# Extra drains on GpSimd, another block order at the end, a smaller first load, and two reorderings in the last turns of a gated scan with a routed expert layer

## The chip, the cores and the metric

One core of a Trainium2 chip runs the whole program. The metric is the device time of one execution in microseconds, and the median of three runs of the kernel before is 382.46 us (382.41 to 382.51). The engines are named as in the profile: PE is TensorE's matmuls, PEld its weight loads, DVE is VectorE, ACT is ScalarE, POOL is GpSimd, SP is SyncE. A q behind a name (POOLq) marks what the engine's sequencer does by itself: waits, branches, drains.

## The reference

A recurrent state with a forget gate for each row, and then a layer of eight experts of which each token uses one.

```python
# q, k, v, f_logit: (4, 8, 768, 48)
f = sigmoid(f_logit)
for t in range(768):
    state = f[:, :, t, :, None] * state + einsum('bhd,bhe->bhde', k[:, :, t], v[:, :, t])
    y[:, :, t] = einsum('bhd,bhde->bhe', q[:, :, t], state)
x = y.transpose(0, 2, 1, 3).reshape(3072, 384)

logits = x @ w_gate                      # 8 experts
e_idx = argmax(logits)
gate_w = softmax(logits)[e_idx]
eom = sigmoid(x @ w_output_gate)
for e in range(8):
    h = maximum(x[e_idx == e] @ w1[e], 0)     # 384 -> 1024
    out[e_idx == e] = gate_w * eom[:, e] * (h @ w2[e])
```

## The kernel before, in words

**The scan.** Four batches of 768 tokens are cut into chunks of 128: 24 turns, one for each chunk, all eight heads together. `prep(t)` makes what turn `t` needs: the sigmoid of the forget gates (`f` and `s`, on ACT), the running product `p` of the gates and its inverse `i` (`scan_p` and `scan_i`, on DVE), and the products `k * i` and `q * p` (`mul_k` and `mul_q`; from turn 3 on both on GpSimd). In turn `t` the function `attention` multiplies k and q of the chunk (`qk`, PE), masks the square (`mask`: one half by DVE, the other by an ACT copy and a GpSimd select), transposes k (`kn_tr`), forms the output of chunk `t - 1` from the state and the masked square (`out_y`), adds the chunk to the state (`state` on PE, `state_upd` on DVE), and transposes the output of chunk `t - 2` into token order together with its gate logits (`x_tr`, PE; `evac_x`, ACT). `evac_y` copies an output from PSUM.

**Loads.** `load(b, cuts)` issues the loads of one batch on SyncE's queue: a cut ("fqk", 0, 2) stands for the gates, q and k of chunks 0 and 1. In the first two batches a load of two chunks has 512 KB, in pieces of 1 KB (256 tokens of 4 bytes). The transfers move in the order in which they are issued.

**Routing.** `route` finds the expert of each token of a group (eight groups, `RG`), by DVE operations that are handed out a few at a time. `slots` counts on PE and DVE where each token goes; `run_pq` runs it. `scatter(n)` then sends up to n chunks of 128 tokens to their places in `xs_dram`, by one indirect DMA each, issued by GpSimd. From turn 20 on (`T_END`) up to four chunks are sent in a turn. Once 16 chunks are sent (`T_TOP`), `tokens_in(0, 0, 2)` loads the first 256 tokens of the largest expert (`first_x`, SyncE); this load waits until those 16 scatters have landed. `x_early` transposes them on PE and splits them into two parts.

**The last turn** (`t == last`) has an order of its own: after `out_y(22)` and `state(22)` it runs the pending slots, sends two chunks, then copies `y` of turn 22, updates the state, does `x_early`, and forms `out_y(23)`, for half of the heads at a time.

**The experts.** `Experts.run` takes the experts in order of size, the largest first. Weights are loaded by SyncE when a buffer is free and split into a high and a low part; each product is three matmuls (`mm1` from 384 to 1024, `mm2` back). For experts 0 to 5 the output of expert s is transposed, scaled by ACT and scattered to `out` during expert s + 1 (`put`, four blocks). Experts 6 and 7 use `mm2_rows`: three blocks of up to 128 tokens, of which each is scaled (half by ACT, then half by DVE, since the second reads the same PSUM bank) and scattered at once. So 30 output blocks are scattered. Every scatter is an indirect DMA of GpSimd and waits for the landing of the one before, since both write to `out`. The scaled blocks have three buffers.

**The end.** `check` counts whether the fast method was valid, into the register `bad`. `tc.If(bad > 0)` would run `general_path`, a slow method for all tokens; with these inputs it is skipped. Behind it comes the closing code (recorded on line 1130): every engine drains, SyncE waits for the outstanding DMAs one by one, and GpSimd releases a barrier of all engines.

**What sets the order.** Each engine runs its instructions in the order in which the program writes them (`chain` ties the order of DVE, ACT, GpSimd and PE); SyncE's queue is in the order of its calls.

Of the kernel before, what the change touches and what calls it, by code (L numbers as in the profile page):

```python
# [13 lines left out]
AF = mybir.ActivationFunctionType  # L14
ALU = mybir.AluOpType
# [112 lines left out]
def attention(ctx, tc, nc, k, kpool, rt, q01, k01, f01, q23, k23, f23, v, wg, xs_dram, r, ex):  # L128
# [40 lines left out]
    def load(b, cuts):  # L169
        i = b % 2  # L170
        if b not in v_t:
            v_t[b] = vp.tile([128, NCH, H * 64], F32, name="v_t")
        src = {"f": (f_t[i], f01, f23), "k": (k_t[i], k01, k23), "q": (q_t[i], q01, q23)}
        for what, c0, c1 in cuts:
            sl = slice(c0 * C, c1 * C)
            for w in what:
                if w == "v":
                    nc.sync.dma_start(out=v_t[b][:, c0:c1, :], in_=v[b, sl].rearrange("(c p) h e -> p c (h e)", p=C))
                    continue
                t, first, rest = src[w]  # L180
                if b < 2:
                    nc.sync.dma_start(out=t[:, :, sl], in_=first[b, :, :, sl].rearrange("g p s -> p g s"))
                else:
                    for par in range(2):
                        nc.sync.dma_start(out=t[64 * par:64 * par + D, :, sl],
                                          in_=rest[b - 2, par::2, :, sl].rearrange("h d s -> d h s"))
# [171 lines left out]
    def run_pq(n=None):  # L358
        n = len(pq) if n is None else n
        todo, pq[:] = pq[:n], pq[n:]  # L360
        for f in todo:
            f()
# [58 lines left out]
    order = [(b, c) for b in range(B) for c in range(NCH)]  # L421
    last = len(order) - 1
    pre_of = [prep(t) for t in range(len(order))]
    load(0, [("fqk", 0, 2), ("f", 2, 4), ("v", 0, 2), ("qk", 2, 4)])
    nc.sync.dma_start(out=turn[:, 0::2, 2 * D:XW], in_=wg[:, 0::2, 0:2 * E])
    for i in range(2):
        nc.sync.dma_start(out=turn[64 * i:64 * i + 64, 1::2, 2 * D:XW],
                          in_=wg[64 - 64 * i:128 - 64 * i, 1::2, 0:2 * E])
    load(0, [("v", 2, 4), ("fkqv", 4, 6)])
    load(1, [("fkqv", 0, 2), ("fkqv", 2, 4), ("fkqv", 4, 6)])  # L430
    for e in range(E):
        ex.clear(e)
# [29 lines left out]
    for t in range(last + 1):  # L462
        ready = len(pq)
        more = 1 if t < T_END else 0

        fill(more)
        if hot(t - 2):
            evac_y(t - 2, (1,))
        if t not in (0, 2):
            pre(t + 2, "f")  # L470
        if hot(t - 2):
            evac_y(t - 2, (0,))
            state_upd(t - 2)
        if t == 2:
            pre(4, "f")
        pre(t + 1, "mul_k")
        if t + 1 == last:
            done_sb.close()
            ex.open_early()
        fill(more)  # L480
        if t > 1:
            pre(t + 2, "scan_p")
        qk(t)
        mask(t, 1)
        mask(t, 0)
        if t == 0:
            pre(2, "s", "f")
        pre(t + 2, "scan_p", "scan_i")
        if t == 0:
            pre(2, "mul_k")  # L490
        fill(more)
        kn_tr(t)
        if t == 0:
            warm_up(nc, k, one, 4)
        if hot(t - 2):
            x_tr(t - 2)
        evac_kn(t)
        pre(t + 2, "mul_q", "ends")
        if hot(t - 2):
            evac_x(t - 2)  # L500
        if t == last:
            ex.split(1, 0, 1, nc.gpsimd)
        fill(more)
        if T_END <= t < last:
            fill(8)
        pre(t + 3, "s")
        if t == last:
            done_ps.close()
            ex.open_early_psum()
        if hot(t - 1):  # L510
            out_y(t - 1)
        if hot(t - 1):
            state(t - 1)
        run_pq(ready)
        if t == last:
            scatter(2)

            evac_y(t - 1)
            state_upd(t - 1)
            ex.x_early()  # L520
            for heads in ((0, 1, 4, 5), (2, 3, 6, 7)):
                out_y(t, heads)
            ex.split(1, 0, 2, nc.gpsimd)
        if t >= T_SCAT:
            scatter(1 if t < T_END else 2)

        b, c = divmod(t - 3, NCH)
        if t >= 3 and b + 2 < B and c in (0, 2, 4):
            load(b + 2, [("fkq", c, c + 2)])
            if c == 4:  # L530
                load(b + 2, [("v", i, i + 2) for i in range(0, NCH, 2)])
        fill(2 if more else 10)
        fill(2 * more)
        if t - 2 in ends:
            route(*ends[t - 2])
        if t >= T_END:
            scatter(2)
            if len(ex.apart) == T_TOP:
                ex.tokens_in(0, 0, EARLY // TS)
                ex.load_rest(0)  # L540
        if t + 1 == last:
            drain()
            assert ex.xg
            ex.split(1, 0, 0, nc.gpsimd)
# [32 lines left out]
class Experts:  # L577
# [208 lines left out]
    def mm2_rows(self, s, step):  # L786

        k, nc = self.k, self.nc
        for j, n in self.rows(s):
            ps = self.psy.tile([128, 512], F32, name=f"y_ps{j}")  # L790
            i = 0
            for f in range(KF):
                wh, wl = self.whl[2, s, f // 2]
                hh, hl = (t[:, j * TS:j * TS + n] for t in self.hs[s, f][0])
                for a, b in ((hh, wh), (hl, wh), (hh, wl)):
                    nc.tensor.matmul(ps[0:n, 0:DM], a, b[:, f % 2, :], start=(i == 0), stop=(i == 3 * KF - 1))  # L796
                    i += 1
                step(j * KF + f)
            t = self.yp.tile([TS, DM], F32, name="o", bufs=3)
            half = DM // 2  # L800
            nc.scalar.activation(out=t[0:n, 0:half], in_=ps[0:n, 0:half], func=AF.Copy,
                                 scale=k.gain[0:n, j, s:s + 1])
            nc.vector.tensor_scalar(out=t[0:n, half:DM], in0=ps[0:n, half:DM], scalar1=k.gain[0:n, j, s:s + 1],
                                    scalar2=None, op0=ALU.mult)
            self.scatter(s, j, n, t)

    def y_out(self, s):
# [56 lines left out]
    def run(self):  # L864
        step = self.step
        step(len(self.todo))
        self.load_rest(1)
        for f in range(AHEAD):
            if f == AHEAD - 2:
                self.x_late()  # L870
            self.mm2(0, f)
        for s in range(E):
            if s > 0 and s + 1 < E:
                self.load(s + 1, self.k.number[0:1, s + 1:s + 2])
            back = self.rows(s - 1) if s > 0 and len(self.rows(s - 1)) > KC else []
            if s == 0:
                later = self.meta.pop()
                self.gains()
                self.meta = [later]
            for f in range(KF):  # L880
                self.mm1(s, f)
                if s == 0:
                    self.gain(2)
                    if f in (3, 5):
                        self.split(1, 1, f // 2 - 1)
                if f % 2 == 0 and (2, s, f // 2) in self.wr:
                    self.split(2, s, f // 2, self.nc.gpsimd if s == 0 else None)
                if 1 <= f <= len(back):
                    self.put(s - 1, *back[f - 1])
            front = [lambda i=i: self.split(1, s + 1, i) for i in range(KF // 2)  # L890
                     if (1, s + 1, i) in self.wr]
            for c in range(KC):
                front.insert(2 * c + 2 if s > 0 else 2 * c + 1, lambda c=c: self.x_in(s + 1, c))
            if s + 1 == E:
                front = []
            self.gain(len(self.gq))
            self.gains()
            if len(self.rows(s)) <= KC:
                self.mm2_rows(s, lambda i: self.gain(1) if i % 3 != 1 else front.pop(0)() if front else None)
                self.gain(len(self.gq))  # L900
                continue
            for f in range(KF):
                for part in range(len(self.hs[s, f])):
                    if not (s == 0 and part == 0 and f < AHEAD):
                        self.mm2(s, f, part)
                if front:
                    front.pop(0)()
                self.gain(2)
                if s == 1:
                    step(1)  # L910
            self.gain(len(self.gq))
            self.y_out(s)
            if s == 0:
                self.todo += check(self.nc, self.k, self.r, self.kp, self.pso)
# [151 lines left out]
def tile_kernel(ctx: ExitStack, tc: tile.TileContext, q01, k01, f01, q23, k23, f23, v, vT, wg, wgn, w1, w2, out):  # L1066
# [20 lines left out]
    def part(first, rest):  # L1087
        return lambda b, h: first[b, h // 2, 64 * (h % 2):64 * (h % 2) + D, :] if b < 2 else rest[b - 2, h]

    with tc.If(bad > 0):  # L1090
        general_path(tc, nc, part(q01, q23), part(k01, k23), part(f01, f23), vT, wgn, w1, w2, y_dram, out)


# [40 lines left out]
```

## Time and profile before

| | us |
|---|---|
| median of the runs | 382.46 |
| the profiled execution's own time | 382.55 |
| its span, first to last instruction | 380.8 |
| PE busy | 361.7 (95%) |
| DVE busy | 234.8 (62%) |
| ACT busy | 196.8 (52%) |
| POOL busy | 146.7 (39%) |

The profile is of one execution. Busy is the time in which an engine worked, waits and branches left out. The chain of waits goes back from the last instruction, at each step to what released it; its shares say where the span was decided. A row of a timeline gives the start and the duration in us, the engine, the line, the operation, the tiles (output <- inputs) and, in brackets, how long the engine was idle before and what ended that.

### The profile page before, as it was taken

Reading aid. Unit: us, or ns where it says so; the run is one execution under the profiler, and the core shown is the slowest. Engines: PE = TensorE matmul, PEld = TensorE weight load, DVE = VectorE, ACT = ScalarE, POOL = GpSimd, SP = SyncE. Lnnn points to the kernel's source line nnn. Section 1 sums busy time; section 2 is a strip of 40 time slices with the busy share of each in tenths; the row PEclk is TensorE's granted clock in tenths of the full one; section 3 lists DMA queues with packets and bytes.
Section 4 is the critical chain, followed back from the end, with each engine's and each line's share of the span. In section 5 each row is a group of like instructions: output and inputs, shape, how many; then the busy total and the mean of one; then the engine's idle time right before and its main releaser. Section 6 shows DMA issues by size and latency. Waiting matters only on the chain.

```text
span 380.8 us, 8463 instructions
## 1 busy us (share of the span) xinstructions
PE 361.7 (95%) x3199; PEld 334.2 (88%) x3199; DVE 234.8 (62%) x488; ACT 196.8 (52%) x468; POOL 146.7 (39%) x176
## 2 busy tenths in 40 slices
PE   7899999999998999999999999999999999999990
PEld 2688988898986999899989999999999999999980
DVE  6988989898974655645535545644653654665410
ACT  3576866866756434446336435625634644744310
POOL 6686698999988630002102201301210211231021
PEclk9999999999999999999999999999999999999996
DMA  8999999999178149545453543545444454420010
GB/s 253 348 359 359 312 252 267 299 269 284 47 244 265 54 148 335 177 133 167 134 170 124 175 126 126 167 127 185 133 162 135 159 166 128 160 66 35 2 43 21
DMA packets 51843, 67.75 MB, mean 178 GB/s; under 512 B 3906, under 2 KB 46421, under 8 KB 51792
## 3 DMA queue, kind: packets, MB, share of 16 engines
q1 hardware_dynamic: 48480, 57.46, 50.6%
q0 software_dynamic: 3312, 9.65, 7.0%
q8 instruction: 27, 0.44, 0.5%
q14 instruction: 24, 0.20, 0.2%
HBM read 54.16 MB, written 13.39 MB: 177 GB/s over the span
## 4 chain that ended last, share of the span: by engine, by line
PE 78%; DVE 9%; ACT 3%; issue 3%; DMA 3%; POOL 2%; POOLq 0%; DVEq 0%; ACTq 0%
PE h_ps L760 28%; PE y_ps L782 22%; PE x_ps L322 5%; PE y_ps L796 4%; PE a_ps L245 3%; PE x_ps L710 3%; PE two_ps L309 2%; DVE p L209 2%; DVE i L216 2%; PE o_ps L817 2%; PE two_ps L305 2%; PE one_ps L309 2%; PE kn_ps L262 2%; PE one_ps L278 2%; DMA out<-o,dst 2%
## 5 line engine op out<-in xcount | busy, mean ns | idle before, releaser
L825 POOL DMA_INDIRECT out<-o,dst x30 | 31.7, 1058 | 187.8 <-ACT o L820 118.6
L765 DVE SCALAR_TENSOR_TENSOR hl<-h_ps,hh 128x256 fp32r<-128x256 f32 (+6 forms) x72 | 39.3, 547 | 51.2 <-ACT hh L764 50.8
L760 PE MATMUL h_ps<-xh,w1h 128*128 128x400 f32 (+6 forms) x192 | 67.4, 351 | 0.3 <-DVE hl L765 0.3
L760 PE MATMUL h_ps<-xh,w1l 128*128 128x400 f32 (+6 forms) x192 | 65.0, 338 | 0.0
L760 PE MATMUL h_ps<-xl,w1h 128*128 128x400 f32 (+6 forms) x192 | 65.0, 338 | 0.0
L764 ACT ACTIVATE hh<-h_ps 128x256 fp32r<-128x256 f32 (+6 forms) x72 | 34.8, 484 | 50.1 <-PE h_ps L760 48.5
L782 PE MATMUL y_ps<-hh,w2h 128*128 128x256 f32 (+4 forms) x168 | 57.7, 343 | 0.0
L782 PE MATMUL y_ps<-hl,w2h 128*128 128x256 f32 (+4 forms) x168 | 55.7, 331 | 0.0
L782 PE MATMUL y_ps<-hh,w2l 128*128 128x256 f32 (+4 forms) x168 | 55.6, 331 | 0.0
L717 DVE TENSOR_TENSOR xl<-x_ps,xh 128x400 fp32r<-128x400 f32 (+6 forms) x23 | 13.1, 569 | 41.8 <-ACT xh L716 38.4
L760 PEld LDWEIGHTS h_ps<-xh,w1h 128*128 128x128 f32 x192 | 36.1, 188 | 1.2 <-DVE hl L765 0.6
L716 ACT CAST xh<-x_ps 128x400 fp32r<-128x400 f32 (+6 forms) x23 | 11.3, 490 | 48.9 <-PE x_ps L710 42.3
L760 PEld LDWEIGHTS h_ps<-xl,w1h 128*128 128x128 f32 x192 | 36.1, 188 | 0.4
L760 PEld LDWEIGHTS h_ps<-xh,w1l 128*128 128x128 f32 x192 | 36.0, 188 | 0.5
L636 DVE TENSOR_TENSOR w2l<-w2r,w2h 128x768 fp32r<-128x768 f32 x31 | 30.7, 989 | 4.2 <-ACT w2h L635 1.3
L223 POOL TENSOR_TENSOR q_t<-q_t,p 128x512 f32<-128x512 f32 x24 | 30.6, 1276 | 6.1 <-DVE p L209 5.9
L245 PE MATMUL a_ps<-q_t,k_t 64*128 64x128 f32 x384 | 28.4, 285 | 4.5 <-DVE k_t L220 2.7
L782 PEld LDWEIGHTS y_ps<-hh,w2h 128*128 128x128 f32 x168 | 31.6, 188 | 1.1
L782 PEld LDWEIGHTS y_ps<-hl,w2h 128*128 128x128 f32 x168 | 31.6, 188 | 0.5
L782 PEld LDWEIGHTS y_ps<-hh,w2l 128*128 128x128 f32 x168 | 31.7, 189 | 0.4
L209 DVE TENSOR_TENSOR_SCAN p<-f_ps,start_p 128x511 f32<-128x511 f32 x22 | 28.0, 1274 | 4.0 <-ACT start_p L197 2.4
L245 PEld LDWEIGHTS a_ps<-q_t,k_t 64*128 64x128 f32 x384 | 23.7, 187 | 7.1 <-POOL q_t L223 2.0
(176 smaller groups left out, 773.4 us busy)
## 6 DMA issues: line engine op xcount, KB each, us to landing
w1r<-in_w SPq DMA_DIRECT2D x32, 384.0 KB, 3.7
w2r<-in_w SPq DMA_DIRECT2D x32, 384.0 KB, 3.2
v_t<-in_v SPq DMA_DIRECT2D x12, 512.0 KB, 8.6
xg<-xs_dram SPq DMA_DIRECT2D x5, 802.0 KB, 5.0
xs_dram<-empty SPq DMA_DIRECT2D x8, 401.0 KB, 10.9
f_t<-in_f SPq DMA_DIRECT2D x6, 512.0 KB
q_t<-in_q SPq DMA_DIRECT2D x6, 512.0 KB, 9.4
k_t<-in_k SPq DMA_DIRECT2D x6, 512.0 KB, 8.6
```

The costliest lines, as they stand in the source:

```text
L209: nc.vector.tensor_tensor_scan(out=flat(d["p"])[:, 1:n], data0=flat(d["f"])[:, 0:n - 1], data1=sp[:, 1:n], initial=sp[:, 0:1], op0=ALU.mul ...
L223: nc.gpsimd.tensor_tensor(out=q_t[i][:, :, sl], in0=q_t[i][:, :, sl], in1=d["p"], op=ALU.mult)
L245: nc.tensor.matmul(aps[t][par][:, g, :], k_t[b % 2][r, g, sl], q_t[b % 2][r, g, sl], start=(g == 0), stop=(g == NP - 1))
L309: nc.tensor.matmul(yps[t][g % 2][r0:r0 + 64, g // 2, :], v_t[b][:, c, 64 * h:64 * h + 64], at[t][:, h % 2, g, :], start=(c == 0 and h < 4) ...
L322: nc.tensor.matmul(xps[t][:, g, :], xt[t][:, g, :], turn[:, g, :], start=(g == 0), stop=(g == NP - 1))
L636: (eng or self.nc.vector).tensor_tensor(out=flat(lo), in0=flat(t), in1=flat(hi.bitcast(F32)), op=ALU.subtract)
L760: nc.tensor.matmul(ps[:, 0:n], a[:, c, cs], b, start=(i == 0), stop=(i == 3 * KC - 1))
L764: nc.scalar.activation(out=hi, in_=ps[:, 0:n], func=AF.Relu)
L765: nc.vector.scalar_tensor_tensor(out=lo, in0=ps[:, 0:n], scalar=0.0, in1=hi.bitcast(F32), op0=ALU.max, op1=ALU.subtract)
L782: self.nc.tensor.matmul(self.ys[d][:, c0:c0 + n], a[:, f % 2, ds], b, start=(f == 0 and i == 0 and part == 0), stop=(f == KF - 1 and i == ...
L796: nc.tensor.matmul(ps[0:n, 0:DM], a, b[:, f % 2, :], start=(i == 0), stop=(i == 3 * KF - 1))
L825: self.nc.gpsimd.indirect_dma_start(out=self.out, out_offset=bass.IndirectOffsetOnAxis(ap=self.k.dst[0:n, j, s:s + 1], axis=0), in_=t[0:n] ...
```

## The change

Six edits. The first load takes chunk 0 alone, then chunks 1 and 2, then 3 and 4, and chunk 5 with the second part. In the last turn the copy of `y(22)` and the state update come ahead of the pending slots and the two scatters. In turns 20 and 21 `mul_k` of turn t + 2 is done ahead of that turn's scatters (it was done at the start of the turn after). `mm2_rows` scales a block with one ACT instruction over all 384 columns. From expert 2 on, GpSimd gets a drain at the start of each expert (six drains). And the conditional block at the end is laid out so that the arm that skips `general_path` comes next in the program.

```diff
@@ -421,12 +421,12 @@
     order = [(b, c) for b in range(B) for c in range(NCH)]
     last = len(order) - 1
     pre_of = [prep(t) for t in range(len(order))]
-    load(0, [("fqk", 0, 2), ("f", 2, 4), ("v", 0, 2), ("qk", 2, 4)])
+    load(0, [("fqk", 0, 1), ("fqk", 1, 3), ("v", 0, 2), ("fqk", 3, 5)])
     nc.sync.dma_start(out=turn[:, 0::2, 2 * D:XW], in_=wg[:, 0::2, 0:2 * E])
     for i in range(2):
         nc.sync.dma_start(out=turn[64 * i:64 * i + 64, 1::2, 2 * D:XW],
                           in_=wg[64 - 64 * i:128 - 64 * i, 1::2, 0:2 * E])
-    load(0, [("v", 2, 4), ("fkqv", 4, 6)])
+    load(0, [("v", 2, 4), ("fkq", 5, 6), ("v", 4, 6)])
     load(1, [("fkqv", 0, 2), ("fkqv", 2, 4), ("fkqv", 4, 6)])
     for e in range(E):
         ex.clear(e)
@@ -511,16 +511,20 @@
             out_y(t - 1)
         if hot(t - 1):
             state(t - 1)
-        run_pq(ready)
-        if t == last:
-            scatter(2)
+        if t < last:
+            run_pq(ready)
+        else:
 
             evac_y(t - 1)
             state_upd(t - 1)
+            run_pq(ready)
+            scatter(2)
             ex.x_early()
             for heads in ((0, 1, 4, 5), (2, 3, 6, 7)):
                 out_y(t, heads)
             ex.split(1, 0, 2, nc.gpsimd)
+        if T_END <= t:
+            pre(t + 2, "mul_k")
         if t >= T_SCAT:
             scatter(1 if t < T_END else 2)
 
@@ -797,11 +801,7 @@
                     i += 1
                 step(j * KF + f)
             t = self.yp.tile([TS, DM], F32, name="o", bufs=3)
-            half = DM // 2
-            nc.scalar.activation(out=t[0:n, 0:half], in_=ps[0:n, 0:half], func=AF.Copy,
-                                 scale=k.gain[0:n, j, s:s + 1])
-            nc.vector.tensor_scalar(out=t[0:n, half:DM], in0=ps[0:n, half:DM], scalar1=k.gain[0:n, j, s:s + 1],
-                                    scalar2=None, op0=ALU.mult)
+            nc.scalar.activation(out=t[0:n], in_=ps[0:n, 0:DM], func=AF.Copy, scale=k.gain[0:n, j, s:s + 1])
             self.scatter(s, j, n, t)
 
     def y_out(self, s):
@@ -872,6 +872,8 @@
         for s in range(E):
             if s > 0 and s + 1 < E:
                 self.load(s + 1, self.k.number[0:1, s + 1:s + 2])
+            if s > 1:
+                self.nc.gpsimd.drain()
             back = self.rows(s - 1) if s > 0 and len(self.rows(s - 1)) > KC else []
             if s == 0:
                 later = self.meta.pop()
@@ -1087,7 +1089,7 @@
     def part(first, rest):
         return lambda b, h: first[b, h // 2, 64 * (h % 2):64 * (h % 2) + D, :] if b < 2 else rest[b - 2, h]
 
-    with tc.If(bad > 0):
+    with tc.If(bad > 0, preferred_fallthrough_block=False):
         general_path(tc, nc, part(q01, q23), part(k01, k23), part(f01, f23), vT, wgn, w1, w2, y_dram, out)
```

## Rows read from the trace of the kernel before

**Rows 1.** The page, part 4: shares of the chain of waits by engine.

```profile
PE 78%; DVE 9%; ACT 3%; issue 3%; DMA 3%; POOL 2%; POOLq 0%; DVEq 0%; ACTq 0%
```

**Rows 2.** Timelines of ACT, DVE and POOL, 369 to 381 us.

```profile
370.53 0.42 ACT L801 ACTIVATE o<-y_ps,gain 120x192 f32<-120x192 f32 x1 [3.73 <-PE y_ps L796]
...
370.99 0.42 DVE L803 TENSOR_SCALAR o<-y_ps,gain 120x192 f32<-120x192 f32 x1 [3.73 <-ACT o L801]
...
372.21 1.03 POOL L825 DMA_INDIRECT out<-o,dst  x1 [3.70 <-DVE o L803]
```

**Rows 3.** Instructions on the tile o, 372 to 381 us: issue to landing.

```profile
DMA to landing us min/median/max: 3.0/3.0/3.0
```

**Rows 4.** Line 1130: op xcount, ns min/median/max, first and last start.

```profile
L1130 POOLq DRAIN  x3: 40/107/4492, 375.5 to 380.6; - x3
...
L1130 SPq DRAIN  x3: 7/7/12, 375.9 to 380.3; - x3
...
L1130 DVEq DRAIN  x2: 10/72/135, 377.3 to 380.3; - x2
```

**Rows 5.** The same view of line 1125, the program's start.

```profile
L1125 POOLq DRAIN  x1: 176/176/176, 0.4 to 0.4; - x1
```

**Rows 6.** Timeline of POOL, 318 to 323 us.

```profile
322.72 1.09 POOL L825 DMA_INDIRECT out<-o,dst  x1 [15.77 <-ACT o L820]
```

**Rows 7.** The view of line 1090, the branch at the end.

```profile
L1090 PEldq COMPARE_BRANCH  x1: 3722/3722/3722, 367.8 to 367.8; - x1
...
L1090 POOLq COMPARE_BRANCH  x1: 53/53/53, 372.5 to 372.5; - x1
...
L1090 POOLq EVENT_SEMAPHORE  x1: 17/17/17, 375.4 to 375.4; - x1
```

**Rows 8.** Chain of waits, 361 to 381 us: start, us, what.

```profile
363.80 2.58 DMA out<-o,dst
...
367.53 3.83 DMA out<-o,dst
```

**Rows 9.** DMA queues, 367.6 to 371.4 us: packets, MB, share.

```profile
q8 instruction: 1, 0.02, 2.1%
```

**Rows 10.** Instructions on the tile o, whole span: ns min/median/max.

```profile
L820 ACT ACTIVATE o<-o_ps,gain x24: 569/578/588, 169.3 to 327.9; 128x384 f32<-128x384 f32 x19, 16x384 f32<-16x384 f32 x2, 64x384 f32<-64x384 f32 x1, 48x384 f32<-48x384 f32 x1
```

**Rows 11.** Chain of waits, 0 to 6 us.

```profile
0.80 4.21 DMA f_t<-in_f
...
5.86 1.29 DVE p L209
```

**Rows 12.** Busy time by stretch; the last number is GB/s.

```profile
5.00:7.50 2.50, 2.50 (x13) 1.15 (x12) 1.57 (x3) 1.93 (x7) 1.19 (x16) 1.00 1.09 354
...
9.00:10.00 1.00, 0.56 (x10) 0.59 (x11) 1.00 (x2) 0.00 (x0) 0.00 (x0) 1.00 1.04 377
```

**Rows 13.** Timelines of DVE and ACT in the first turns.

```profile
9.26 1.27 DVE L209 TENSOR_TENSOR_SCAN p<-two_ps,start_p 128x511 f32<-128x511 f32 x1
...
14.41 0.20 ACT L197 ACTIVATE start_p<-f_t 128x4 f32<-128x4 f32 x1
```

**Rows 14.** Waits, 109 to 116 us: total, times, longest.

```profile
PE a_ps L245 <- POOL k_t L220: 1.5, 2, 0.8
```

**Rows 15.** Timelines of POOL, SP and PE in the last turns.

```profile
107.28 0.98 POOL L339 DMA_INDIRECT xs_dram<-xn,slot  x1 [0.30 <-issue]
...
113.85 1.29 POOL L220 TENSOR_TENSOR k_t<-k_t,i 128x512 f32<-128x512 f32 x1
...
114.40 0.37 SPq L657 DMA_DIRECT2D first_x<-xs_dram  x1
...
119.85 0.63 PE L710 MATMUL x_ps<-ident,first_x 128*128 128x128 f32 x4
...
121.19 0.65 PE L305 MATMUL f_ps<-q_t,state 64*64 64x128 f32 x8 [0.49 <-DVE state L293]
```

**Rows 16.** Instructions on the tile first_x, 114 to 118 us: issue to landing.

```profile
DMA to landing us min/median/max: 5.1/5.1/5.1
```

## The prediction

> **What bounds the kernel now.** I read the chain of waits first, then the sequencers' instructions at the end, then the first 15 us and the last turns of the scan. The chain is TensorE for 78% of the span [rows 1]: from the third turn of the scan to the end of the last expert nothing but a shorter wait of PE can pay. That leaves three places where PE does not set the time: the head (the first forget gates are waited for), the last four turns (PE waits for GpSimd's `k` product), and the tail after PE's last matmul, 370.5 to 380.8 us. The change touches all three.
>
> The tail is the largest. The last ACT and DVE scaling end at 371.4, the last scatter is issued at 372.2 [rows 2] and lands 3.0 us later [rows 3], at 375.2. The program nevertheless runs to 380.8. What lies between is in the sequencers' rows: GpSimd's first DRAIN of the closing line starts at 375.5 and lasts 4.49 us [rows 4], so it ends at 380.0; 0.8 us of closing barrier follow. SyncE was ready at about 376.0: its first DRAIN is at 375.9 [rows 4]. So GpSimd's DRAIN ends last, by 4.0 us.
>
> **The change, part by part.**
>
> *Drains in the experts.* The reader is to compare three DRAINs of GpSimd: 0.18 us at the start of the program [rows 5], 4.49 at the end, and 0.11 and 0.04 right behind that one [rows 4]. A fixed price is excluded; the long one differs by what stands before it, 54 indirect scatters (24 turns and 30 output blocks) that no drain has followed up. An estimate from these rows: 4.49/54 = 0.083 us for each. With a drain at the start of experts 2 to 7, only the three scatters of expert 7 are left to the last one: 3 x 0.083 = 0.25 us, or, if it must see the last scatter land, until just after that landing. The six added drains: the first has 28 scatters behind it, 28 x 0.083 = 2.3 us, the next four have 4 each, 0.3 us, and the one of expert 7 has 7, 0.6 us. Each stands on GpSimd behind the scatters of the expert two back (at expert 7 of the two before it), and the next scatter is far off: GpSimd's pauses between experts are 15.8 us or more [rows 6]. Hidden, 0. Nothing but those scatters is queued behind a drain on GpSimd, and ACT and PE wait for them only through three output buffers. Bounds of the last drain: 0 to 4.49 us; I take the small end, because the two DRAINs that follow the long one are its nearest kin.
>
> The Trainium skill (VectorE: DVE Perf Modes, The DRAIN you can't avoid) holds the drains of the closing code to be about 12 ns, the same on all engines. The trace disagrees by 4.49 us on GpSimd and agrees on SyncE (7 to 12 ns). By that rule the added drains would have nothing to take away; what a constant price does here, at the size that the row shows, is the first rival.
>
> *No jump.* GpSimd's compare-and-branch starts at 372.5 and its next instruction at 375.4 [rows 7]: 2.9 us lost. PE's own branch takes 3.72 us. With the skipping arm laid out next, each engine goes straight on. GpSimd then reaches its last drain at about 372.5 instead of 375.5. This pays only together with a short drain, since SyncE's readiness follows the last landing. A second effect: the next-to-last scatter took 3.83 us against 2.58 of the one before [rows 8], and in its stretch stands one instruction fetch on the DMA engines [rows 9], just while PE's branch was waiting. Without the jump I expect about 2.6.
>
> *One ACT scaling in place of ACT plus DVE.* ACT alone on 384 columns takes 0.58 us [rows 10]; so 370.53 + 0.58 = 371.11 instead of 370.99 + 0.42 = 371.41 [rows 2]: 0.3 us. With the earlier scatter landing at about 369.8 the scaling is last before the final scatter. That scatter starts at 371.4 to 371.9 (0.3 to 0.8 after the scaling; it was 0.8) and lands 2.6 to 3.0 later, 374.0 to 374.9; I take 374.45, 0.8 us before the old 375.2. For expert 6 the same edit costs nothing: PE uses other banks.
>
> Tail: landing 374.45, SyncE ready 0.75 later as before, barrier 0.8: 376.0 instead of 380.8, **4.8 us** less (4.3 to 5.3).
>
> *First chunk alone.* The first load of `f` (512 KB, 1 KB pieces) lands at 0.80 + 4.21 = 5.01, and the first scan starts 0.85 later [rows 11]. Halving it makes pieces of 512 B, which no row shows. Two rates bracket it: 354 GB/s with 1 KB pieces, 377 with 2 KB [rows 12]; over 16 engines a piece of 1 KB takes 46.3 ns and one of 2 KB 86.9, so 512 B is about 26 ns on that line. 32 pieces an engine: 0.83 instead of 1.48 us, 0.65 saved on `f`. It holds if the later chunks come in time. The transfers run in the order of issue; counted from 5.01 - 1.48 = 3.53: three small ones (2.5), `f` of chunks 1 and 2 (1.48): lands at 7.5, scan of chunk 1 possible at 8.4, wanted at 9.26 - 0.65 = 8.6. Then `q`, `k` (2.96), `v` (1.4), `f` of chunks 3 and 4 (1.48): 13.4, wanted at 14.41 - 0.65 = 13.8 [rows 13]. Both in time, with 0.2 and 0.4 to spare. SyncE issues three more DMAs, and the gate weights behind them are wanted only at the first transposition of `x`, two turns on. Bounds: with a proportional price 0.75; if 512 B took as long as 1 KB, `f` of chunk 1 would land at 9.4 and the scans be 1.1 later. I take **0.6** less, and PE carries it on.
>
> *Last turns.* The `k` product of turns 22 and 23 goes ahead of turn 20's three and turn 21's two scatters. PE had waited 1.5 us for it, in two waits [rows 14]. With `k` early, and the state update of turn 22 ahead of the slots, PE could be at its last `out_y` (121.19) some 2 us sooner. But the scatters move back by one `k` product, 1.29 us, and the third of turn 20 (107.28) is the sixteenth, for which SyncE holds the load of `first_x` (issued 114.40) [rows 15], which lands 5.1 later, at 119.5 [rows 16]. The early transpositions stand ahead of `out_y` in PE's order: landing, 0.1 of wait, six transpositions, which start 0.11 apart (four take 0.63 with the last one's 0.27 [rows 15]), 0.66. So `out_y` can start at 120.25 + s, where s is what the load is later: gain 0.95 - s. s lies between 0 (the scatter queue, slowed by the weight loads, makes it up) and 1.29. I take 0.75, as the queue catches up when the weight loads end: **0.2** less (0.95 less to 0.35 more). GpSimd has the same work in another order, so its masks of turns 22 and 23 end when they did, and PE, which had wanted them later than that, now wants them at about that time: no gain beyond this one could follow.
>
> Sum: 4.8 + 0.6 + 0.2 = 5.6, against the profiled execution's own 382.55 (span 380.8 and 1.7 around it): 376.95. The median of the runs is 0.09 lower: **376.9**. A measurement tells 0.2% (0.76 us) from no change.
>
> **Rivals.**
> 1. *The last drain keeps its price* (a fixed sweep of all queues once anything was scattered). The constant of the Trainium skill is of this kind, at another size. For it: one long drain is all that the trace has. Against: the shorter ones. It then starts at 372.5 instead of 375.5 and ends at 377.0; end 377.8; tail 3.0 less; 382.46 - 3.8 = 378.7.
> 2. *The long drain waits for something after the last landing* (it began 0.3 after it and ended 4.8 after). Then only the 0.8 of the landing is won: 382.46 - 1.6 = 380.9; with poor ends of the other two terms, no change.
> 3. *The jump stays, or the code behind it is fetched late all the same*: GpSimd 375.5, DVE's drain at 377.3 as now [rows 4], end 378.2: 382.46 - 2.6 - 0.8 = 379.1.
> 4. *512 B pieces cost like 1 KB*: 376.9 + 0.6 + 1.1 = 378.6.
> 5. *Slower*: the added drains hold GpSimd longer than its pause. Place: the first scatter of the experts from 2 on. From about 13 us on (15.8 less the landing that the pause already waits out) each drain delays scatters, the three buffers, ACT, then PE. At 15 us: 6 x 2 = 12 more, 382.46 + 12 - 5.6 = 388.9. Against it: the longest drain seen, behind 54 scatters, took 4.49.
>
> **Numbers.** Forecast 0.67 (its own range 375.9 to 377.9: the tail 4.3 to 5.3, the head and the last turns); rivals 0.14, 0.05 (of it 0.02 within 0.2%), 0.06, 0.04, 0.04. The range 375.9 to 379.1 takes in nearly all of the forecast, rivals 1 and 4 and half of 3. Faster 0.94, same 0.02, slower 0.04.
>
> **What would show it.** Right: GpSimd's last drain under 1 us or ending within 0.3 of the last landing, the first of the six about 2.3 us and the others 0.3 to 0.6; under 0.2 us between GpSimd's branch and its next instruction; the next-to-last scatter landing in about 2.6; the first scan at about 5.2; PE's qk of turns 22 and 23 without a wait for `k`, and `first_x` landing later within its turn. Wrong: a last drain of 4.5, a first added drain as long as the others, the scan of chunk 1 not earlier than 9.26, or `out_y` of the last turn more than 0.4 later than the head's gain allows.

## The result, and the profile after

The changed kernel takes 378.47 us in the median against 382.41 of before in the same comparison, ratio 0.9896 (0.987 to 0.9922): 3.9 us less, where 5.6 were forecast. In this comparison the kernel before repeats within 0.2 us, the changed one does not: 377.25, 378.16, 378.47 and 380.42. (A fifth time, 384.33, fell in a disturbed state of the chip and is not used.) Its profiled execution is the one of 380.42, the slowest of the four. A second series, on the chip of group three below, gave 377.97 to 378.94, median 378.84, with a profile of 378.94. Where both stand against the profile of before, in us from the span's start (qk is the product of k and q that opens a turn):

| place | before | after, first | after, second |
|---|---|---|---|
| qk of turn 0 | 9.44 | 8.79 | 8.40 |
| qk of turn 1 | 13.23 | 13.05 | 13.89 |
| qk of turn 13 | 68.31 | 68.18 | 69.05 |
| qk of turn 14 | 72.35 | 74.20 | 73.08 |
| qk of turn 21 | 104.02 | 105.88 | 104.76 |
| qk of turn 23 | 115.20 | 115.31 | 116.37 |
| first matmul of the experts | 124.59 | 127.13 | 125.74 |
| end of PE's last matmul | 370.50 | 373.05 | 371.62 |
| end of the span | 380.84 | 378.71 | 377.23 |

So the tail gives 4.7 us in both (10.34 behind PE's last matmul, then 5.66 and 5.61), and the work ahead of it is later than before, by 2.55 and 1.12 us.

**The tail.** The chain of waits of the changed kernel, 340 to 381 us (start, us, what):

```profile
366.07 3.25 DMA out<-o,dst
...
370.10 2.59 DMA out<-o,dst
...
373.76 0.51 POOLq L1087
374.27 0.79 POOL out L825
```

Its closing line, its conditional block and its added drains (op xcount, ns min/median/max, first and last start):

```profile
L1132 POOLq DRAIN  x3: 46/107/392, 377.2 to 378.4; - x3
L1132 SPq DRAIN  x3: 7/7/13, 377.8 to 378.1; - x3
```

```profile
L1092 PEldq COMPARE_BRANCH  x2: 95/2012/3930, 370.4 to 373.2; - x2
L1092 ACTq COMPARE_BRANCH  x2: 37/43/49, 373.7 to 373.9; - x2
L1092 POOLq COMPARE_BRANCH  x2: 41/44/48, 374.3 to 374.5; - x2
```

```profile
L876 POOLq DRAIN  x6: 3025/4088/5031, 184.3 to 348.7; - x6
```

Against [rows 4]: the 4.49 us drain is 0.39. SyncE's DRAIN at 377.8 now comes after it (377.2 + 0.4), so the last landing (374.03 + 3.1 = 377.1) ends the program. The middle scatter takes 2.59 again, not 3.83 [rows 8]. But each engine now has two branches: the first is passed at once (GpSimd 374.3, next instruction 374.4), behind the second its drain starts only 2.7 us later, and PE's second lasts 3.93 us. The jump has moved, not gone. GpSimd's pause ends close to the landing in every profile; that it is late code and not the landing is read from ACT, which has no scatter to wait for and pauses as long (373.9 to 376.8).

**The head.** The chain, 0 to 20 us:

```profile
2.40 5.84 DMA f_t<-in_f
8.26 0.60 ACT two_ps L204
8.86 0.14 ACT start_p L197
9.02 1.29 DVE p L209
```

`f` of chunk 0 lands at 3.71 instead of 5.01, but `f` of chunks 1 and 2 only at 8.24, and the scan of chunk 1 starts at 9.02, 0.24 before [rows 13]'s 9.26 (in the second profile at 9.87, 0.6 behind it). The reader is to look at the rate of the DMA engines while the small pieces move and as they end (stretch, busy time of PE, PEld, DVE, ACT, POOL with counts, clock, DMA share, GB/s; first of the changed kernel, then of e1_tail below, which has the old loads):

```profile
2.60:3.40 0.80, 0.80 (x4) 0.25 (x3) 0.74 (x2) 0.00 (x0) 0.80 (x3) 1.00 1.12 321
...
4.20:5.00 0.80, 0.80 (x3) 0.30 (x2) 0.44 (x1) 0.52 (x3) 0.73 (x5) 1.00 0.87 204
5.00:5.80 0.80, 0.80 (x3) 0.30 (x2) 0.80 (x1) 0.00 (x0) 0.80 (x12) 1.00 0.85 251
```

```profile
4.20:5.00 0.80, 0.80 (x3) 0.29 (x2) 0.00 (x0) 0.00 (x1) 0.73 (x4) 1.00 1.10 387
5.00:5.80 0.80, 0.80 (x4) 0.34 (x3) 0.04 (x1) 0.77 (x3) 0.80 (x12) 1.00 1.10 350
```

(387 + 350 - 204 - 251) x 0.8 = 226 KB were not moved there: 0.6 us of a full stream, as much as was to be gained. The small loads themselves are not slow: in the first of these stretches, with 512 B pieces alone, they move 321 GB/s. The hole stands where the last of them end and the pieces of 1 KB take over.

**Turn 13.** PE's timeline, 66 to 77 us: PE waits for `v`, which comes from the same stream (issued 63.7, against 62.6 before). The kernel before has no such row.

```profile
72.73 0.44 PE L309 MATMUL two_ps<-at,v_t 128*64 128x128 f32 x4 [1.92 <-DMA v_t<-in_v]
```

**The last turn.** Timeline of SyncE and PE, 116 to 127 us, and the stretches of it:

```profile
117.05 0.37 SPq L661 DMA_DIRECT2D first_x<-xs_dram  x1
...
120.36 0.17 PE L408 MATMUL two_ps<-ohb,upper 128*128 128x16 bf16 x1 [0.74 <-ACT xt L316]
...
121.48 0.63 PE L714 MATMUL x_ps<-ident,first_x 128*128 128x128 f32 x4 [0.90 <-DMA first_x<-xs_dram]
...
122.84 1.12 PE L309 MATMUL f_ps<-at,v_t 128*64 128x128 f32 x8
```

```profile
120.00:122.00 2.00, 0.74 (x8) 0.68 (x8) 0.97 (x4) 0.31 (x2) 1.83 (x3) 1.00 0.98 296
122.00:124.00 2.00, 2.00 (x21) 1.33 (x21) 0.97 (x3) 1.32 (x4) 1.70 (x2) 0.69 1.06 396
124.00:126.00 2.00, 2.00 (x17) 1.34 (x17) 1.79 (x9) 1.16 (x2) 1.77 (x2) 0.50 1.01 374
```

Both waits for `k` [rows 14] are gone: from qk of turn 21 to that of 23 it is 9.43 us instead of 11.18. Then PE idles 0.74 us for ACT's copy (the slots now stand behind it and share its PSUM bank) and 0.90 for `first_x`, is busy 0.74 of 2 us, and the granted clock falls from 1.0 to 0.5, the level of 1.2 GHz: eight matmuls of `f_ps` take 1.12 us instead of 0.66 at full clock. From qk of turn 23 to the experts it is 11.82 us; before it was 9.39.

### The profile page after: what moved, and what is told of

Same layout as the page of the kernel before. It is cut to its first block, busy times and chain, and to the rows that moved or that the text cites. A ratio compares the mean times of both kernels' runs of the same rounds, so it can differ in the third digit from the quotient of the medians.

```text
span 378.7 us, 8460 instructions
## 1 busy us (share of the span) xinstructions
PE 364.1 (96%) x3199; PEld 335.5 (89%) x3199; DVE 232.2 (61%) x482; ACT 198.0 (52%) x468; POOL 145.8 (38%) x176
## 4 chain that ended last, share of the span: by engine, by line
PE 76%; DMA 8%; DVE 7%; ACT 3%; issue 3%; POOL 1%; SPq 0%; POOLq 0%; DVEq 0%; ACTq 0%
PE h_ps L764 28%; PE y_ps L786 22%; PE y_ps L800 4%; PE x_ps L322 4%; PE x_ps L714 3%; PE a_ps L245 3%; DMA v_t<-in_v 2%; PE two_ps L309 2%; PE o_ps L817 2%; PE one_ps L309 2%; DMA xs_dram<-xn,slot 2%; PE two_ps L305 2%; DVE p L209 2%; DVE i L216 2%; DMA f_t<-in_f 2%
## 5 line engine op out<-in xcount | busy, mean ns | idle before, releaser
L825 POOL DMA_INDIRECT out<-o,dst x30 | 30.7, 1025 | 187.9 <-ACT o L820 120.6
L640 DVE TENSOR_TENSOR w1l<-w1r,w1h 128x768 fp32r<-128x768 f32 x28 | 26.8, 956 | 4.4 <-ACT w1h L639 3.5
```

What stands on the lines that cost most here:

```text
L640: (eng or self.nc.vector).tensor_tensor(out=flat(lo), in0=flat(t), in1=flat(hi.bitcast(F32)), op=ALU.subtract)
L825: self.nc.gpsimd.indirect_dma_start(out=self.out, out_offset=bass.IndirectOffsetOnAxis(ap=self.k.dst[0:n, j, s:s + 1], axis=0), in_=t[0:n] ...
```

## The experiments

Runs of one group were on one chip and share the times of the kernel before: e1 to e4 382.18, e5 to e10 382.39, e12 to e16 382.22; the three groups were on three chips. Theory A is the reading above; each rival has its letter.

**Group one: the change in parts.** e1_tail has the three edits of the tail alone; e2 adds the loads, e3 the last turns, e4 takes the block's layout back.

> The kernel before with the three edits of the tail alone (six drains, the skipping arm next, one ACT scaling); loads and last turns as before. Theory A (the tail gains what the changed kernel shows, 10.3 - 5.65 = 4.65 us behind PE's last matmul; the loss and the spread of the times come from the loads and the last turns): 382.4 - 4.65 = 377.75, all times within 0.5 us, no PE wait for v, TensorE clock 1.0 in the last turn. Rival B (the drains or the new layout disturb the queues or the clock): the times spread over 2 us or more here too, or PE's last matmul ends over 0.5 us later than the 370.5 of before.

377.47 us (377.43 to 377.51), ratio 0.9878 (0.9862 to 0.9893). Theory A; B falls: PE's last matmul ends at 370.26, the clock in the last turn is 1.0, and the times are tight. The tail is worth 4.7 us by itself, more than the whole change.

```diff
-    load(0, [("fqk", 0, 2), ("f", 2, 4), ("v", 0, 2), ("qk", 2, 4)])
+    load(0, [("fqk", 0, 1), ("fqk", 1, 3), ("v", 0, 2), ("fqk", 3, 5)])
-    load(0, [("v", 2, 4), ("fkqv", 4, 6)])
+    load(0, [("v", 2, 4), ("fkq", 5, 6), ("v", 4, 6)])
```

> The tail's edits and the new load order; last turns as before. Theory A: the 512 B pieces make the stream of loads late, and v of the third batch lands after PE wants it in turn 13: the second qk starts 0.2 us earlier than before, turn 14 up to 2 us later; 377.75 - 0.2 + (0 to 1.9) = 377.5 to 379.4, with the times spread over 1 us or more. Rival C (the wait for v was chance, the load order only gains): 377.5, spread under 0.5.

378.0 (377.93 to 379.12): 0.5 slower than e1_tail. Turn 1 starts at 13.21 (13.12 in e1_tail). Later ACT waits for gates and PE 0.2 us for `v`; turn 11 starts at 59.49 instead of 59.15. The row of ACT, first of e2 (timeline, 54 to 60 us), then of e1_tail, where the same wait is 1.0 us shorter:

```profile
54.73 0.21 ACT L197 ACTIVATE start_p<-f_t 128x4 f32<-128x4 f32 x1 [1.59 <-DMA f_t<-in_f]
```

```profile
53.74 0.21 ACT L197 ACTIVATE start_p<-f_t 128x4 f32<-128x4 f32 x1 [0.60 <-DMA f_t<-in_f]
```

So the loads cost time; C falls. The wait of 1.92 for `v` did not return in this size.

```diff
-        run_pq(ready)
-        if t == last:
-            scatter(2)
+        if t < last:
+            run_pq(ready)
+        else:
             evac_y(t - 1)
             state_upd(t - 1)
+            run_pq(ready)
+            scatter(2)
             ex.x_early()
...
+        if T_END <= t:
+            pre(t + 2, "mul_k")
```

> The tail's edits and the new last turns; loads as before. Theory A: the qk of the last turn starts 1.5 us sooner (two waits for k gone), but PE then idles over 1.5 us before the transposition of first_x, and its granted clock falls to 0.5 for some 3 us behind it, which costs about 1.4 us: mm1 starts within 1 us of where it did before (124.6); 377.75 + 0 to 1, times spread. Rival D (no fall of the clock when the v wait is not there): the gain of the k waits less the later first_x remains, 376.5 to 377.5, and the clock reads 1.0.

376.55 (375.5 to 378.21): 0.9 less than e1_tail, and spread. The profile is of 375.5 and shows rival D's case: qk of turn 23 at 112.87 (114.95 in e1_tail), and in PE's timeline, 117 to 119 us, no wait for `first_x`:

```profile
117.93 0.17 PE L408 MATMUL two_ps<-ohb,upper 128*128 128x16 bf16 x1 [0.74 <-ACT xt L316]
...
118.04 0.63 PE L714 MATMUL x_ps<-ident,first_x 128*128 128x128 f32 x4
```

The load was issued at 114.30 and landed in 3.2 us, not in the 5.1 of [rows 16]; clock 1.0. The slower executions of e3 have no profile; that the clock falls in them is not shown.

```diff
-    with tc.If(bad > 0, preferred_fallthrough_block=False):
+    with tc.If(bad > 0):
```

> As e1_tail, with the conditional block laid out as in the kernel before (the jump stays). Theory A: the layout only moves the late fetch of code behind the second branch, where the last landing covers it; without it the closing drains start as late as before, 3 us behind the branch, and the landing still ends last: at most 0.5 us slower than e1_tail. Rival E (the prediction's: DVE's and GpSimd's drains come 3 us later and end last): 1.5 us or more slower than e1_tail. In both the next-to-last scatter lands in about 3.8 us and not in 2.6.

377.66 (377.59 to 378.25), 0.2 slower than e1_tail. Theory A; E falls. The middle scatter lands in 3.62 us (2.58 in e1_tail), as both said, and the last one is issued 1.39 us behind PE's last matmul (0.98 in e1_tail).

**Group two: the price of a drain, and two cures.** e5 leaves the six drains out, e7 keeps three.

```diff
-            if s > 1:
-                self.nc.gpsimd.drain()
```

```diff
-            if s > 1:
+            if 1 < s < 5:
                 self.nc.gpsimd.drain()
```

> As e1_tail without the six drains in the experts. Theory H (a drain takes about 0.083 us for each scatter that no drain has followed up, once the last one has landed): the last drain begins at the landing, about 374.4 on the scale of e1_tail, lasts 4.5 us again and ends last: 377.47 + 4.1 = 381.5. Rival I (the long drain of before was the late code behind the jump, not the scatters): 377.5 to 378.

> As e1_tail, but drains only in experts 2, 3 and 4: 18 scatters are left to the last drain. Theory H (proportional): last drain 18 x 0.083 = 1.5 us behind the landing in place of 0.39, of which about 0.25 is covered by SyncE's own waits: 377.47 + 0.85 = 378.3. Rival J (a fixed price, paid when the last drain is long ago or none went before): 377.5 with a drain of 0.4, or 381.5 with one of 4.5.

381.58 (381.35 to 381.94, and once 384.76) and 378.7 (378.56 to 378.89). Without the drains the tail's other two edits are worth 0.8 (382.39 before). The closing line's drains, first of e5, then of e7, then of e1_tail:

```profile
L1126 POOLq DRAIN  x3: 40/107/4563, 374.5 to 379.6; - x3
```

```profile
L1128 POOLq DRAIN  x3: 46/107/1609, 374.7 to 376.9; - x3
```

```profile
L1128 POOLq DRAIN  x3: 46/107/393, 374.4 to 375.5; - x3
```

54 scatters not followed up: 4.56 us (4.49 before); 18: 1.61; 3: 0.39 (0.30 in e4). (4.56 - 1.61)/36 = 0.082 and (1.61 - 0.39)/15 = 0.081 us for each, with 0.15 left over: a straight line, for drains that begin after the last landing. H is shown for these; I and J fall. The middle one was worked out from one row ahead of the run (1.5). GpSimd's other work does not count: 115 more of its instructions stand ahead of the 54 than ahead of the 18, at the same price for a scatter. Whether the scatters count or the rows in them is not told apart.

e9 is the changed kernel with `v` of the third and fourth batch moved ahead; e10 is e3 with the transposition of `first_x` moved back.

```diff
+            if c == 4:
+                load(b + 2, [("v", 0, 2)])
             load(b + 2, [("fkq", c, c + 2)])
             if c == 4:
-                load(b + 2, [("v", i, i + 2) for i in range(0, NCH, 2)])
+                load(b + 2, [("v", i, i + 2) for i in range(2, NCH, 2)])
```

```diff
             scatter(2)
-            ex.x_early()
-            for heads in ((0, 1, 4, 5), (2, 3, 6, 7)):
-                out_y(t, heads)
+            out_y(t, (0, 1, 4, 5))
+            ex.x_early()
+            out_y(t, (2, 3, 6, 7))
```

> The changed kernel with one load moved: the first v of each later batch goes ahead of that batch's last load of f, k and q. Theory A (the new load order makes the stream late, and v of turn 12 was what PE waited for): no wait of PE for v in turn 13, median 376.6 to 377.4 in place of 378.47. Rival C (the v wait was chance, the loss is elsewhere): 378 or more, or the same wait for v again.

378.68 (378.22 to 379.39): a miss, and rival C's number. The wait for `v` is not there (PE goes on at 70.69), and yet the median does not fall. A stall came in that no run of group one has: PE, timeline 109.3 to 110.2 us,

```profile
109.33 0.18 PE L408 MATMUL two_ps<-ohb,upper 128*128 128x16 bf16 x1 [0.41 <-issue]
109.37 0.19 PE L410 MATMUL two_ps<-ohb,ones 128*128 128x16 bf16 x2
110.06 0.41 PE L245 MATMUL a_ps<-q_t,k_t 64*128 64x128 f32 x2 [0.50 <-issue]
```

"issue" is a wait for nothing that the profile shows. It begins at the same place, late in turn 21 while the first expert's weights are being loaded, in all eight profiles of groups two and three (in e9 and e16 it comes again ahead of qk of turn 23, 0.41 us), and in none of the six before. The loading alone does not bring it: e3, without it, moves 180 to 340 GB/s from 106 to 114 us. No instruction fetch stands in it either: the queues for instructions moved nothing in e9 from 106 to 112 us. In e5 and e7 it costs nothing, since the waits for `k` cover it (11.20 and 11.16 us from qk of turn 21 to that of 23); in e9, where they are gone, those turns take 11.55, against 9.42 in e3. Of these 2.1 us the rows named issue show 1.3; the rest is matmuls that follow one another more slowly (the sixteen of L278 take 1.00 us, 0.62 in the changed kernel's first profile).

> As e3_tail_turns, with the transposition of first_x between the two halves of the last out_y, so that PE has 1.2 us more work before it needs that load. Theory A (the spread of e3_tail_turns is PE idle before first_x and the fall of the clock behind it): 375.3 to 376.3 in all runs, spread under 1 us. Rival K (the spread comes from elsewhere, the weights or the clock by itself): 375.5 to 378.2 as before.

379.48 (379.45 to 379.66): tight, but over 3 us above what I expected. Rival K named the spread, and there is none. The stall of turn 21 is here too (11.09 us for turns 21 and 22), and PE has no idle ahead of `first_x`. But the splits of `first_x` on ACT and DVE start 4.1 us later than in e3 (122.84, not 118.75; 1.7 of it from turns 21 and 22) and hold the gate work behind them; PE, 126 to 127 us:

```profile
126.26 0.17 PE L408 MATMUL two_ps<-ohb,upper 128*128 128x16 bf16 x1 [1.03 <-DVE ohb L385]
```

So the early transposition leads a chain over ACT and DVE here; it isn't filler for PE.

**Group three: smaller edits, and the change again.** e12 has the tail and the order of the last turn, without the `k` products; e14 adds that of turn 23 alone, e15 to it a smaller first load.

```diff
-        if T_END <= t:
-            pre(t + 2, "mul_k")
```

```diff
+        if t == T_END + 1:
+            pre(t + 2, "mul_k")
         if t >= T_SCAT:
```

```diff
-    load(0, [("fqk", 0, 2), ("f", 2, 4), ("v", 0, 2), ("qk", 2, 4)])
+    load(0, [("f", 0, 1), ("f", 1, 2), ("qk", 0, 2), ("f", 2, 4), ("v", 0, 2), ("qk", 2, 4)])
```

> As e1_tail with the order of the last turn alone changed (copy and state update ahead of the slots and two scatters); the k products stay where they were. Theory A (the moved k products bring both the gain and the spread of e3_tail_turns): 377.0 to 377.4, all times within 0.5 us; the two waits for k stay (0.7 and 0.8 us), the 0.5 us wait for the state goes. Rival M (the state update is what gains): 376.6 or less.

377.82 (377.76 to 378.56). No gain: 0.74 for ACT's copy stands where 0.49 for the state stood, and the last turn takes 9.68 us instead of e1_tail's 9.40. Theory A's 377.0 to 377.4 was 0.4 too low; M falls.

> As e12_tail_state, with the k product of turn 23 alone ahead of turn 21's scatters; that of turn 22 stays behind turn 20's three, so that the sixteenth scatter and with it the load of first_x are not delayed. Theory A: the 0.8 us wait before the last qk goes, first_x is issued where e1_tail has it (113.7), PE does not wait for it: 376.3, within 1 us in all runs. Rival N (taking PE's wait away only moves it to first_x or to the instruction supply): 377 or more, or a spread of over 1.5 us as in e3_tail_turns.

377.88 (377.61 to 378.05). `first_x` is issued at 113.6 and not waited for, as theory A said, but the gain isn't there: the stall has taken the place of the wait (PE, waits of 100 to 127 us: total, times, longest). Rival N.

```profile
PE two_ps L309 <- issue: 0.8, 2, 0.5
PE two_ps L408 <- ACT xt L316: 0.7, 1, 0.7
```

> As e14_state_k23, with a smaller change of the first loads: only f of chunks 0 and 1 is loaded alone, each 256 KB; q and k stay in pairs. Theory A (three small loads in a row left the DMA engines half empty from 4 to 5.6 us, and six of 512 B pieces made the stream late): f of chunk 0 lands 1.2 us sooner, f of chunk 1 before 5.5, the second qk starts 0.3 to 0.6 sooner, no wait for v: 0.4 less than e14_state_k23, about 375.9. Rival L (any smaller first piece is paid back in the stream): not less than e14_state_k23.

378.67 (378.39 to 378.88): 0.8 slower than e14. `f` of chunk 0 came 0.8 earlier (ACT 3.96, e14 4.77), but q and k of the pair behind it came late; GpSimd, 7 to 9.5 us:

```profile
8.06 1.26 POOL L223 TENSOR_TENSOR q_t<-q_t,p 128x512 f32<-128x512 f32 x1 [2.08 <-DMA q_t<-in_q]
```

and turn 0 starts at 10.28 (9.11). Rival L. The stream falls again, here behind two small loads, and not while they move: the stretch below holds 141 packets with 0.14 MB, pieces of 1 KB, and the 512 B pieces ahead of it moved 343 GB/s (2.6 to 3.4). So it does not need three small loads in a row, and it is not that small loads move slowly.

```profile
4.20:5.00 0.80, 0.80 (x3) 0.30 (x2) 0.28 (x1) 0.77 (x4) 0.73 (x5) 1.00 0.67 180
```

> The changed kernel again, for a second profile of it. Theory A: its times spread over more than 1 us again around 378 to 379, and the profile shows where its own time comes from: behind a time of 378 or more stand a wait for v, PE idle in turns 21 to 23 or a granted clock of 0.5 in the last turn; behind one of 377.3 or less none of them. Rival O (the first five times were a chance of that chip): 376.0 to 376.9, tight.

378.84 (377.97 to 378.94); O falls. In its profile `f` of chunks 1 and 2 lands still later (ACT's row below), turn 1 starts 0.66 after that of before; no wait for `v`, no fall of the clock, but the stall: turns 21 and 22 take 11.61 us, and the last turn 9.37.

```profile
9.11 0.60 ACT L204 ACTIVATE two_ps<-f_t 128x508 f32<-128x508 f32 x1 [4.14 <-DMA f_t<-in_f]
```

## Why the prediction was right, and where it was not

**The closing drain: right in mechanism and size.** The tail was put at 4.8 us (4.3 to 5.3); e1_tail gives 4.7 by its run times and the profiles 4.7. The 0.083 us for each scatter, taken from one row, is 0.082 over three points. Rival 1 is out by e7, rival 2 by the drain's end 0.5 after the landing. The Trainium skill (VectorE: DVE Perf Modes, The DRAIN you can't avoid) gives about 12 ns for the drains of the closing code, on every engine. SyncE's 7 to 13 ns agree with it; GpSimd's 0.39, 1.61 and 4.56 us do not, and the measurement decides. The landing, which the one ACT scaling and the faster middle scatter were to bring 0.8 sooner, came 0.7 to 0.8 sooner behind PE's last matmul (4.74 us before, 4.08 in the changed kernel, 3.96 in e1_tail), and 0.6 with the jump left in (4.17 in e4); the scaling was not run alone.

**The six added drains: misread, hidden.** I expected 2.3 us for the first and 0.3 to 0.6 for the rest; they last 5.03 and 3.0 to 4.5. Each was issued right behind a scatter and waits for its landing too: 307.61 + 4.1 = 311.7 for one, which ends at 307.43 + 4.48 = 311.9. What is left beyond the landing is 0.20 with 4 scatters, 0.33 with 7 and 1.20 with 28 (landing 188.1, end 189.3), within 0.01 in e1 to e4 too, where the profile has these landings: again a straight line, but with 0.042 us for each, half the price of the closing drain. Why half is open; that a part of the follow-up goes on while the last scatter is still under way would fit, and is not shown. By the letter of "a first drain as long as the others" the proportion would have been called wrong. GpSimd's pause of 15.8 us [rows 6] hid them all, as stated.

**No jump: half right.** The first branch is passed in 0.1 us, but a second one follows, with 2.7 us on GpSimd. It costs nothing, because the landing ends later: rival 3's late code without its price. Taken alone the layout is worth 0.2 us (e4), by the profiles through the middle scatter, behind which the last one is issued 0.4 sooner.

**First chunk alone: the step that failed.** It was to give 0.6, from 26 ns a piece and a stream that is always full. The piece was right (27 ns in the median of the first 20 us), the small loads moved 321 GB/s, and chunk 0 was 1.0 to 1.3 us earlier, more than the 0.65 forecast, since the old first load had not moved at the full rate that I counted back with (95 GB/s from 1.8 to 2.6 us, 154 from 2.6 to 3.4). But the stream was not full: at 4.2 to 5.8 us, where the last small loads end and the pieces of 1 KB take over, it moved 204 and 251 GB/s where the large loads moved 387 and 350, in e2 240 and 309, in e16 198 and 222. So `f` of chunks 1 and 2, put at 7.5, landed at 8.2 to 9.1, and turn 1, which I took as following, started from 0.2 sooner to 0.7 later. I had bounded the price of a piece and not the change from small loads to large ones; what makes the hole there is open. Chunk 5 alone (three more small loads), which I did not price, keeps the stream late: from 18 to 26 us e2 and the changed kernel move 2.74 and 2.72 MB, e1 2.87, and e15, with small first loads but chunk 5 in its pair, 2.86. What waits for the stream is gates or `v` 40 to 60 us on. Together the 0.6 to be gained became 0.5 lost (e2 against e1).

**Last turns: right place, wrong size, and not the same everywhere.** The sum said 0.95 - s with s = 0.75. On the first chip it was 0.9, in the best execution 2.0: the 5.1 us of `first_x` that capped it is 3.2 in e3 and 4.3 in the changed kernel, so it was no constant. The state's place gave nothing: 0.74 for a copy replaced 0.49, since the slots' products share a PSUM bank with `y(22)`, a wait that I had not looked for. Where `first_x` comes late, 0.9 of wait and about 1.5 of fallen clock (11.82 - 9.37 - 0.90) take the gain. On the other two chips the stall of turn 21 took it: with the waits for `k` turns 21 and 22 take 11.16 to 11.20 us there (e5, e7, e12), and without them 11.55 and 11.61 (e9, e16); e3 on the first chip, and the first profile, have 9.42.

**Sum.** 4.7 by the tail, -0.5 by the loads, and -0.4 (11.2 - 11.6 in e9 and e16) to +0.9 (e3 against e1) by the turns, leave 3.8 to 5.1 if the parts simply added; 3.9 and 3.4 were measured, at the low end and below it. The wait for `v` and the fallen clock are in the first profile, the stall in the second; which of them stands behind each single time is open, as is the cause of the stall. That the time lay inside the range is luck: the forecast's own part ended at 377.9, and the range reached further for the sake of rivals 1, 3 and 4 (378.6 to 379.1), none of which happened: the drain did not keep its price, the late code cost nothing, and a 512 B piece took 27 ns.

The fastest version measured is e3 (376.55, spread 2.7 us, on one chip); the steadiest fast one is e1_tail. The spreads are to be read with care: in the three groups the kernel before, too, runs from 381.66 to 382.99, with single times of 385.2 and 385.85. That e3 would beat e1_tail on the other two chips was not tried, and e14 and e16 speak against it.

## What to carry to other kernels

Before a kernel with many GpSimd scatters ends, let a drain stand where GpSimd pauses anyway: what the closing drain must follow up then shrinks with the number left. A wait that is removed shows its price only with what it covered, here a stall without a releaser and a load that the idle engine was early for; look for that in several executions. And a first load cut in half is worth its time only if the loads right behind it still keep the DMA engines full.

## What was not expected of the hardware

- A drain of GpSimd that begins after the last landing costs 0.082 us for each earlier scatter that no drain has followed, and 0.15 besides. One that begins before it waits for it, and then has 0.042 us left for each.
- Loads of 256 KB in pieces of 512 B moved at 318 to 343 GB/s (2.6 to 3.4 us), but where they end, from 4.2 to 5.8 us, the stream fell to 180 to 310, though 512 KB loads were already issued; without the small ones it moved 350 to 387.
- PE stood 0.5 to 1.3 us "on issue" in turns 21 and 22 in eight profiles on two chips, in none of four on a third; where no wait for `k` stood there, the two turns were 1.6 to 2.2 us longer than without it.
